# Two loads of an attention decode step, cut differently: W_down's last 96 rows as 93 + 3, the first K as four pieces

## The chip, the cores and the metric

The kernel runs on one core of one Trainium2 chip. The metric is the device time of one execution in microseconds, taken as the median of several executions. The time before is 661.27 us, the median of three runs (660.88 to 662.06).

## The reference

One decode step of a transformer block for two sequences (B = 2, one token each, D = 512): a layer norm, attention with 32 heads of 128 over a cache of 8192 positions, a residual, another layer norm, and a feed-forward part with a ReLU gate. All inputs are bf16.

```python
def _A_ref(x, k_cache, v_cache, wq, wo):              # k_cache, v_cache: (2, 32, 8192, 128)
    q = (x @ wq).reshape(B, Sq, Hq, Dh).transpose(0, 2, 1, 3)
    scores = einsum("bhqd,bhkd->bhqk", q, k) * (Dh ** -0.5)
    p = softmax(scores)
    o = einsum("bhqk,bhkd->bhqd", p, v)
    return o.transpose(0, 2, 1, 3).reshape(B, Sq, Hq * Dh) @ wo

def _B_ref(x, W_gate, W_up, W_down):                  # (512, 1376), (512, 1376), (1376, 512)
    gate = x @ W_gate
    gate = gate * (gate > 0)
    return (gate * (x @ W_up)) @ W_down

h = x + _A_ref(layernorm(x), k_cache, v_cache, wq, wo)
h2 = h + _B_ref(layernorm(h), W_gate, W_up, W_down)
```

(The function bodies are shortened; the output is h2, 2 x 512 in bf16.) The two caches are 256 MB together, and every byte of them is used once.

## The kernel before

**Steps.** The attention runs in N = 32 steps, each with one sequence and two heads. A step loads a K block and a V block of 4 MB each: the 16,384 rows of 128 numbers of two heads, laid on 128 partitions with 128 rows each, so that a partition gets one contiguous stretch of 32 KB. There are two buffers of each kind (`kbuf`, `vbuf`), used in turn. K0 below is the K block of step 0, V31 the V block of step 31.

**A step.** VectorE multiplies the K block with the query, which stands repeated on all partitions (L320), adds up the 128 products by halving (L338, four additions) and a last sum (L342), takes the maximum of each partition (L350) and, after TensorE has spread it (L352), the maximum over the partitions (L276). ScalarE sums 8 of the 128 columns instead of VectorE (L329) and makes the exponentials (L279). TensorE multiplies them with the V block (L378, or L367 in the last two steps). Step 0 multiplies its K block in two halves, so that the first half can start when half of the block is there; for that the load is cut into two pieces (L149, `pieces=2` of `load_kv`, L124 to L131).

**The order of the loads.** All loads but that of x are issued by SyncE (SP), in one queue, in the order of the program. At the front stand W_q (4 MB, into `wbig`), K0 in two pieces, K1 and V0; then in each step i the K block of step i + 2 and the V block of step i + 1 (L396 to L401). Each of these waits for its buffer: a K load for VectorE's last sum of the step that used the buffer, a V load for TensorE. The instructions keep their order, so that a load that waits holds back those behind it. A load also waits for the landing of the eighth load before it, since the loads take turns on eight semaphores.

**The end.** After V31 come W_o in three loads (L412; 2 MB, 1 MB, 1 MB, into `wbig`), W_gate and W_up (L421, 1376 KB each, into the free half of `kbuf`), and W_down. Of W_down's 1376 rows, 1280 lie in `wd_sb`, loaded in three pieces of 768, 256 and 256 KB (L425, with 6, 2 and 2 KB for a partition, in rows of 2 KB), and the last 96 (`LASTW`) in a tile of their own, `wd_r`, one row of 1 KB on a partition (L430). Behind the last step, TensorE multiplies with W_o (L464), W_gate and W_up (L500) and W_down (L533: ten chunks of `wd_sb`, then `wd_r` with four matmuls); VectorE copies the result (L538), TensorE brings it into rows and adds the residual (L539), VectorE rounds it (L541), and SP stores y (L542).

Of the kernel before, what the change touches and what calls it, by code (L numbers as in the profile page):

```python
# [13 lines left out]
def _free(t, offset, dims):  # L14

    return bass.AP(tensor=t.tensor, offset=t.offset + offset, ap=[t.ap[0]] + [list(d) for d in dims])


def _dram(t, offset, dims):
    return bass.AP(tensor=t.tensor, offset=t.offset + offset, ap=[list(d) for d in dims])  # L20
# [3 lines left out]
def kernel(  # L24
# [13 lines left out]
    nc = tc.nc  # L38
    P = nc.NUM_PARTITIONS
    B, Sq, D = A_x.shape  # L40
# [20 lines left out]
    FULL = F // (2 * P) * 2  # L61
    LASTW = F - FULL * P
# [20 lines left out]
    kbuf = big.tile([P, 2, ROW], bf16)  # L83
# [3 lines left out]
    wd_r = big.tile([P, D], bf16)  # L87
# [36 lines left out]
    def load_kv(cache, buf, i, pieces=1):  # L124
        b, g = steps[i]
        w = ROW // pieces
        for k in range(pieces):
            nc.sync.dma_start(  # L128
                out=buf[:, i % 2, k * w:(k + 1) * w],
                in_=_dram(cache, (b * Hkv + 2 * g) * Sk * Dh + k * w, [[ROW, P], [1, w]]),  # L130
            )  # L131
# [13 lines left out]
    with tc.manual_schedule():  # L145

        nc.sync.dma_start(out=wq_all, in_=_dram(A_wq, 0, [[KC * Hq * Dh, P], [1, KC * Hq * Dh]]))  # L147
        nc.scalar.dma_start(out=xrow[0:B, :], in_=_dram(A_x, 0, [[D, B], [1, D]]))
        load_kv(A_k_cache, kbuf, 0, pieces=2)  # L149
        load_kv(A_k_cache, kbuf, 1)  # L150
        load_kv(A_v_cache, vbuf, 0)

# [33 lines left out]
        for c in range(KC):  # L186
            nc.tensor.matmul(
                out=x_ps[:, c, :], lhsT=xrow[0:B, bass.DynSlice(c, P, step=KC)], rhs=ident[0:B, 0:B],
# [13 lines left out]
            out=xn.rearrange("p c b -> p b c"), in0=dev, in1=_free(rstd, 0, [[1, B], [0, KC]]), op=ALU.mult,  # L202
# [204 lines left out]
        for (h0, m, blocks, k, loads), n in zip(SETS, rows):  # L407
            r0 = h0 * Dh
            for p0, w in blocks:
                r = 0  # L410
                for nr in loads:
                    nc.sync.dma_start(  # L412
                        out=wbig[p0:p0 + w, off + r * D:off + (r + nr) * D],
                        in_=_dram(A_wo, (r0 + r) * D, [[n * D, w], [1, nr * D]]),
# [9 lines left out]
        for w in WD:  # L424
            nc.sync.dma_start(  # L425
                out=wd2[:, k0:k0 + w, :],
                in_=_dram(B_W_down, k0 * 2 * P * D, [[2 * D, P], [2 * P * D, w], [1, 2 * D]]),
            )
            k0 += w
        nc.sync.dma_start(out=wd_r[0:LASTW], in_=_dram(B_W_down, FULL * P * D, [[D, LASTW], [1, D]]))  # L430

        scores(N - 1)
        powers(N - 1)
# [6 lines left out]
        for k, (h0, m, blocks, _, _) in enumerate(SETS):  # L440
# [4 lines left out]
            for b in range(B):  # L445
# [4 lines left out]
                for p0, w in blocks:  # L450
                    mb = w // q
                    nc.vector.tensor_tensor(
                        out=_free(sp, p0, [[q, mb], [1, q]]), in0=_free(ocol, h1 * B + b, [[B, mb], [0, q]]),
# [5 lines left out]
        for k, (h0, m, blocks, _, _) in enumerate(SETS):  # L459
            n = rows[k]  # L460
            pn = sum(blocks[-1])
            for r in range(n):
                for c in range(KC):
                    nc.tensor.matmul(  # L464
                        out=att_ps[:, c, :],
# [18 lines left out]
            out=hx, in0=_free(hc, 0, [[1, KC], [KC, B], [0, KC]]), in1=_free(quarter, 0, [[0, KC], [0, B], [1, KC]]),  # L484
# [22 lines left out]
        for c in range(KC):  # L507
            nc.tensor.matmul(
                out=y_ps[0:B * KC, bass.DynSlice(c, P // KC, step=KC)],
# [8 lines left out]
        for r, f in parts:  # L518
            nf = f.stop - f.start
            nc.vector.scalar_tensor_tensor(  # L520
                out=gate[r, f, :], in0=g_ps[r, f, :], scalar=0.0, in1=_free(rvar[r], 0, [[0, nf], [1, B]]),
# [8 lines left out]
        for fc in range(FC):  # L530
            w, src = (P, wd_sb[:, fc, :]) if fc < FULL else (LASTW, wd_r[0:LASTW])
            for c in range(KC):
                nc.tensor.matmul(  # L533
                    out=d_ps[:, :, c], lhsT=src[:, c * P:(c + 1) * P], rhs=hm[0:w, fc, :],
# [38 lines left out]
```

## Time and profile before

| what | value |
|---|---|
| median of three runs | 661.27 us (660.88 to 662.06) |
| the profiled execution | 661.32 us |
| its span, first to last instruction | 659.5 us |
| DVE busy | 591.8 us (90%) |
| PE busy | 334.4 us (51%) |
| ACT busy | 142.2 us (22%) |
| SP's DMA queue q1 | 281.06 MB, 99.0% of 16 engines' span |
| mean rate over the span | 427 GB/s |

The span is what the profile covers; the 1.8 us between it and the execution's own time lie around the first and the last instruction. "Busy" is the time in which an engine executed something. The share of q1 is the time that its packets took, over the span of the 16 DMA engines of the core. A load is cut into packets, one for each contiguous stretch, and the trace has the start, length and bytes of each packet, but not the engine that carried it. On a DMA engine the packets run one after the other.

### The profile page before, as it was taken

To read this page: it belongs to the slowest core of one execution; us is meant where nothing else is said; L and a number is where in the kernel's file an instruction comes from. 1 tells how busy PE (TensorE), PEld (TensorE's weight loads), DVE (VectorE), ACT (ScalarE), POOL (GpSimd) and SP (SyncE) were. 2 spreads that over 40 slices of the span, in tenths; PEclk is the share of its full clock that TensorE was granted. 3 is DMA by queue.
4 is the path that set the end of the run, shared out by engine and by line. 5 is a ranking of instruction groups with operands and counts; after the bars stand their busy time and mean duration, and the time that the engine had idled before them with its cause. 6 is when DMAs were issued, how large, how long until landed. Compare 5 with 4: busy or idle time off the path is not lost.

```text
span 659.5 us, 4819 instructions
## 1 busy us (share of the span) xinstructions
PE 334.4 (51%) x1745; PEld 137.2 (21%) x1745; DVE 591.8 (90%) x302; ACT 142.2 (22%) x695; POOL 6.1 (1%) x35
## 2 busy tenths in 40 slices
PE   2135567653355564435665443665445455553565
PEld 1012222211121221111221111222112122121365
DVE  0899999999999999999999999999999999999941
ACT  2222232222202222211222220122222022222310
POOL 3000000000000000000000000000000000000000
PEclk9998887676778766678776668877677887667855
DMA  8999999999999999999999999999999999999996
GB/s 370 435 435 445 417 441 432 426 441 426 433 438 425 439 433 426 444 423 435 434 427 441 425 434 441 421 439 428 431 443 423 435 441 421 441 424 433 444 409 260
DMA packets 11068, 281.37 MB, mean 427 GB/s; under 512 B 1218, under 2 KB 1316, under 8 KB 1956
## 3 DMA queue, kind: packets, MB, share of 16 engines
q1 hardware_dynamic: 11040, 281.06, 99.0%
q8 instruction: 14, 0.23, 0.1%
q14 instruction: 10, 0.08, 0.0%
q10 hardware_dynamic: 4, 0.00, 0.0%
HBM read 281.05 MB, written 0.00 MB: 426 GB/s over the span
## 4 chain that ended last, share of the span: by engine, by line
DMA 49%; DVE 48%; PE 2%; issue 0%; SPq 0%; ACT 0%; DVEq 0%; ACTq 0%
DMA kbuf<-in_A_k_cache_dram 44%; DVE kbuf L320 23%; DVE kbuf L338 21%; DMA vbuf<-in_A_v_cache_dram 3%; DVE scol L342 3%; DMA kbuf<-in_B_W_down_dram 3%; PE po L378 1%; DVE nm L276 1%; DVE pm L350 0%; ACT pgz L279 0%; SPq L128 0%; PE d_ps L533 0%; SPq L147 0%; PE y_ps L539 0%; DVE y L541 0%
## 5 line engine op out<-in xcount | busy, mean ns | idle before, releaser
L378 PE MATMUL po<-vbuf,pgz 128*8 128x512 bf16 x960 | 273.6, 455 | 264.0 <-ACT pgz L279 264.0
L320 DVE TENSOR_TENSOR kbuf<-kbuf,qrep 128x16384 bf16<-128x16384 bf16 (+2 forms) x33 | 277.2, 8400 | 32.0 <-DMA kbuf<-in_A_k_cache_dram 32.0
L338 DVE TENSOR_TENSOR kbuf<-kbuf 128x7680 bf16<-128x7680 bf16 (+4 forms) x128 | 258.9, 2023 | 3.3
L378 PEld LDWEIGHTS <-pgz 128*8 128x8 bf16 x960 | 92.8, 99 | 435.9 <-ACT pgz L279 263.7
L279 ACT ACTIVATE pgz<-scol,nm 64x128 bf16<-64x128 f32 x64 | 27.9, 436 | 246.6 <-DVE nm L276 246.2
L329 ACT ACTIVATE whole<-kbuf 128x128 f32<-128x128 bf16 x256 | 75.3, 295 | 8.0 <-DVE kbuf L320 7.3
L383 ACT ACTIVATE ob<-po 8x512 f32<-8x512 f32 x30 | 17.6, 587 | 202.3 <-PE po L378 202.3
L329 ACT ACTIVATION_READ_ACCUMULATOR whole<-kbuf 128x1 f32 x256 | 47.8, 187 | 0.0
L342 DVE TENSOR_REDUCE scol<-kbuf 128x120 f32<-128x960 bf16 (+1 forms) x32 | 36.8, 1149 | 1.1
L352 PE MATMUL mx_ps<-nscale,pm 128*128 128x128 f32 x64 | 15.8, 330 | 22.7 <-DVE pm L350 22.6
L352 PEld LDWEIGHTS mx_ps<-nscale,pm 128*128 128x128 f32 x64 | 10.0, 196 | 33.0 <-issue 28.6
L210 PE MATMUL q_ps<-wbig,xn 128*2 128x512 bf16 x32 | 10.7, 469 | 8.3 <-DMA wbig<-in_A_wq_dram 8.3
L279 ACT ACTIVATION_READ_ACCUMULATOR pgz<-scol,nm 64x1 f32 x64 | 11.7, 183 | 0.0
L350 DVE TENSOR_REDUCE pm<-scol 128x1 f32<-128x128 f32 x32 | 9.1, 284 | 2.5
L388 PE MATMUL o_ps<-sel,ob 128*128 128x8 f32 (+1 forms) x64 | 8.4, 258 | 5.5 <-ACT ob L383 5.5
L276 DVE TENSOR_REDUCE nm<-mx_ps 128x2 f32<-128x128 f32 x32 | 9.1, 284 | 0.9 <-PE mx_ps L352 0.9
L214 ACT ACTIVATE qrow<-q_ps 2x512 bf16<-2x512 f32 x8 | 4.7, 586 | 24.2 <-PE q_ps L210 24.2
L388 PEld LDWEIGHTS o_ps<-sel,ob 128*128 128x128 f32 x64 | 7.7, 191 | 9.5 <-ACT ob L383 8.3
L367 PE MATMUL o_ps<-pgz,vbuf 128*128 128x2 bf16 x256 | 7.1, 165 | 5.1 <-ACT whole L329 5.1
L367 PEld LDWEIGHTS <-vbuf 128*128 128x128 bf16 x256 | 7.2, 105 | 5.2 <-DMA vbuf<-in_A_v_cache_dram 5.2
L218 PE MATMUL r_ps<-qrow,pick 2*64 2x256 bf16 x32 | 3.9, 321 | 5.4 <-ACT qrow L214 5.4
L263 DVE RECIPROCAL rz<-o_ps 128x8 f32<-128x8 f32 (+2 forms) x10 | 1.9, 189 | 5.2 <-PE o_ps L367 5.2
(88 smaller groups left out, 64.0 us busy)
## 6 DMA issues: line engine op xcount, KB each, us to landing
vbuf<-in_A_v_cache_dram SPq DMA_DIRECT2D x32, 4096.0 KB, 29.2
kbuf<-in_A_k_cache_dram SPq DMA_DIRECT2D x31, 4096.0 KB, 20.3
wbig<-in_A_wq_dram SPq DMA_DIRECT2D x1, 4096.0 KB, 12.1
kbuf<-in_A_k_cache_dram SPq DMA_DIRECT2D x2, 2048.0 KB, 18.7
wbig<-in_A_wo_dram SPq DMA_DIRECT2D x1, 2048.0 KB, 24.2
wbig<-in_A_wo_dram SPq DMA_DIRECT2D x2, 1024.0 KB, 28.2
kbuf<-in_B_W_gate_dram SPq DMA_DIRECT2D x1, 1376.0 KB, 30.9
kbuf<-in_B_W_up_dram SPq DMA_DIRECT2D x1, 1376.0 KB, 33.9
```

The costliest lines, as they stand in the source:

```text
L210: nc.tensor.matmul(out=q_ps[0:B, :], lhsT=xn[:, c, :], rhs=wq_sb[:, c, n * 512:(n + 1) * 512], start=(c == 0), stop=(c == KC - 1),)
L276: nc.vector.tensor_reduce(out=nm, in_=mx_ps, axis=AXIS.X, op=ALU.min)
L279: nc.scalar.activation(out=pgz[r, s, :, j], in_=scol[r, :], func=ACT.Exp, scale=SCALE, bias=nm[r, j:j + 1], accum_out=zc[r, b, g, j:j + 1],)
L320: nc.vector.tensor_tensor(out=kv, in0=kv, in1=_free(qrep, (b * NG + g) * Dh, [[0, n], [1, Dh]]), op=ALU.mult,)
L329: nc.scalar.activation(out=whole, in_=kt[:, t * Dh:(t + 1) * Dh], func=ACT.Copy, accum_out=scol[:, t:t + 1],)
L338: nc.vector.tensor_tensor(out=lo, in0=lo, in1=_free(kt, half, [[Dh, nv], [1, half]]), op=ALU.add,)
L342: nc.vector.tensor_reduce(out=scol[:, 0:nv], in_=_free(kt, 0, [[Dh, nv], [1, 8]]), axis=AXIS.X, op=ALU.add,)
L352: nc.tensor.matmul(out=mx_ps.rearrange("p a b -> p (a b)"), lhsT=_free(pm, 0, [[0, P]]), rhs=nscale, start=True, stop=True,)
L367: nc.tensor.matmul(out=o_ps[e][:, 2 * k:2 * k + 2], lhsT=vbuf[:, s, t * Dh:(t + 1) * Dh], rhs=pgz[:, s, t, :], start=(t == 0), stop=(t == ...
L378: nc.tensor.matmul(out=po[e][r, :], lhsT=_free(pgz, s * NT * 2 + u * T4 * 2, [[1, 2 * T4]]), rhs=vbuf[:, s, u * T4 * Dh:(u + 1) * T4 * Dh] ...
L383: nc.scalar.activation(out=ob[r, :], in_=po[e][r, :], func=ACT.Copy)
L388: nc.tensor.matmul(out=o_ps[e][:, 0:2 * n], lhsT=ob[:, t * Dh:(t + 1) * Dh], rhs=sel[:, t, 0:n, :], start=(t == 0), stop=(t == T4 - 1),)
```

## The change

The first K block is loaded in four pieces of 1 MB instead of two of 2 MB. The last 96 rows of W_down are loaded in two loads of 93 and 3 rows instead of one of 96. The buffers, the computation and the order of all other loads stay as they are; the first multiplication of step 0 now needs two landings, so does the second, and so do the four matmuls with `wd_r`. The lines behind the second edit move down by four.

```diff
@@ -146,7 +146,7 @@
         nc.sync.dma_start(out=wq_all, in_=_dram(A_wq, 0, [[KC * Hq * Dh, P], [1, KC * Hq * Dh]]))
         nc.scalar.dma_start(out=xrow[0:B, :], in_=_dram(A_x, 0, [[D, B], [1, D]]))
-        load_kv(A_k_cache, kbuf, 0, pieces=2)
+        load_kv(A_k_cache, kbuf, 0, pieces=4)
         load_kv(A_k_cache, kbuf, 1)
         load_kv(A_v_cache, vbuf, 0)
@@ -427,7 +427,11 @@
             k0 += w
-        nc.sync.dma_start(out=wd_r[0:LASTW], in_=_dram(B_W_down, FULL * P * D, [[D, LASTW], [1, D]]))
+
+        for r0, w in ((0, 93), (93, 3)):
+            nc.sync.dma_start(
+                out=wd_r[r0:r0 + w], in_=_dram(B_W_down, (FULL * P + r0) * D, [[D, w], [1, D]]),
+            )
```

## Prediction

> **What bounds the kernel now.** I read the busy times and the slices of the span first, then the chain of waits, then the last stretch by windows of 0.5 us and in order of time. The page says which resource is full:
>
> ```profile
> DMA  8999999999999999999999999999999999999996
> q1 hardware_dynamic: 11040, 281.06, 99.0%
> DMA 49%; DVE 48%; PE 2%; issue 0%; SPq 0%; ACT 0%; DVEq 0%; ACTq 0%
> SPq L128 <- DVE scol L342: 538.8, 30, 19.2
> ```
>
> SP's one queue keeps the 16 DMA engines at 99.0% of the span, so 281 MB of loads set the pace. DVE is 90% busy, but SP waits for DVE (538.8 us in 30 waits) with the next transfer already queued, and in the chain of waits, in order of time, DVE runs without a wait from 22.64 to 110 us and from then on waits for each K load to land:
>
> ```profile
> 1.72 20.90 DMA kbuf<-in_A_k_cache_dram
> 22.64 4.44 DVE kbuf L320
> ...
> 110.65 19.84 DMA kbuf<-in_A_k_cache_dram
> ...
> 635.81 19.41 DMA kbuf<-in_B_W_down_dram
> 655.22 0.04 issue
> 655.26 0.49 PE d_ps L533 x12
> ```
>
> So a nanosecond added to every DMA engine early is a nanosecond at the end, and what lands last before 655.26 sets the end. The last stretch in order of time (start, us, engine, line, tiles):
>
> ```profile
> 654.06 1.01 PE L533 MATMUL d_ps<-hm,kbuf 128*128 128x2 bf16 x32 [0.39 <-DMA kbuf<-in_B_W_down_dram]
> 655.26 0.37 PE L533 MATMUL d_ps<-hm,kbuf 128*128 128x2 bf16 x8 [0.19 <-DMA kbuf<-in_B_W_down_dram]
> 655.50 0.25 PE L533 MATMUL d_ps<-hm,wd_r 96*128 96x2 bf16 x4
> 655.78 0.17 DVE L538 CAST d<-d_ps 128x8 bf16<-128x8 f32 x1 [1.84 <-PE d_ps L533]
> ```
>
> PE waits for the last 256 KB piece of W_down until 655.26 and takes the 96 rows of wd_r at 655.50 without a wait: they were issued at 640.57 and landed 14.8 us later, at 655.4. Their slack is 0.1 us. Only what follows (d, y, the store at 656.62) lies behind.
>
> The windows (busy us of each engine with counts, then PE's clock, the DMA share, GB/s) show that the 16 DMA engines don't finish together:
>
> ```profile
> 650.50:651.00 0.50, 0.50 (x8) 0.40 (x5) 0.00 (x0) 0.00 (x0) 0.00 (x0) 0.50 1.01 402
> 652.50:653.00 0.50, 0.50 (x25) 0.50 (x23) 0.00 (x0) 0.00 (x0) 0.00 (x0) 0.50 0.59 227
> 654.00:654.50 0.50, 0.44 (x16) 0.44 (x17) 0.00 (x0) 0.00 (x0) 0.00 (x0) 0.50 0.43 162
> 654.50:655.00 0.50, 0.50 (x22) 0.49 (x19) 0.00 (x0) 0.00 (x0) 0.00 (x0) 0.50 0.23 80
> ```
>
> 0.59 of 16 is about nine engines still at work, 0.43 is seven. The packet records (start, length and bytes of each packet, without the engine's number) give the same: the 1 KB packets of wd_r come in sixteen runs of six. Six runs start at 651.7 to 652.2 (span time), three at 653.1 to 653.5, and seven late ones at 654.4, five times about 654.8, and 655.15.
>
> **The change, part by part.**
>
> *K0 in four loads.* On one engine, consecutive packets of one load start 607 ns apart for 16 KB, 306 ns for 8 KB and 1209 ns for 32 KB, with 6 ns more between two loads. K0 gives each engine 8 rows of 32 KB: now 2 x (8 x 607 + 6) = 9,724 ns, then 4 x (8 x 306 + 6) = 9,816 ns. That is +0.09 us on every engine, and with the queue full it goes to the end. Bounds: 0, if a pause further on swallows it, to +0.09; I take +0.09. The two added issues on SP cost 1.45 / 3 = 0.48 us each, so K1 and V0 are issued 1.0 us later, at about 3.2 and 3.7 us; W_q's load runs until 12.5 us and K0's until 22.6 ahead of them, which covers it. Without that cover it would be 1.0 us of empty queue. DVE's two first multiplications (L320) wait for two landings each instead of one, the later of which is 0.05 and 0.09 us later than now (17.83 and 22.64); DVE's lead is spent by 110.65, so this costs nothing at the end.
>
> *The waits that shift.* Each load waits for the landing of the eighth load before it. Two more loads at the front move the pairing of the next few loads only: K2 then also waits for W_q and all four pieces of K0, landed by 22.6, and it can't be issued before DVE frees its buffer at 36.59 anyway; V1 waits for x's load, done at 2.1; K3, V2, K4 and V3 wait for a piece of K0 where they waited for W_q, x or K0. From K5 on each load is paired as before. At the end the three W_down pieces wait for K31, V30 and V31, and wd_r's load for the first W_o load, as now. The new 3-row load waits for the second W_o load, and the store of y for the third one instead of the second. SP's wait for the second ended at 643.0, and PE's for the third at 645.45. So the 3-row load is issued at 643.0 to 643.4, over 8 us before any engine comes to it, and only the store (656.62) is queued behind it on SP. Cost 0.
>
> *wd_r in 93 and 3 rows.* Here is the cost. In the records every load gives all its engines the same number of rows: 8 of 128, 6 of 96. Equal shares of 93 whole rows are 31 on three engines or 93 on one. I take three, the nearest to what a load does now, and three for the 3 rows too. Rows of 1 KB start 42 ns apart on an engine. So the three engines get 31 x 42 + 6 + 42 = 1.35 us instead of 6 x 42 = 0.25, and the other thirteen get nothing. For an engine of the early nine this ends by 653.5 + 1.35 = 654.9, before PE comes to these rows at 655.50: cost 0. For the late seven it ends at 655.75, about 656.15, or 656.5; with 0.09 from landing to PE (as the last W_down piece: records 655.17, PE 655.26) PE starts at 655.85, 656.25 or 656.6 instead of 655.50: +0.35, +0.75 or +1.1. The gain on the thirteen relieved engines is bounded by the slack, under 0.1 us, since wd3's landing keeps PE at 655.26. Lower bound of the part 0, upper bound (93 rows on one late engine, 93 x 42 = 3.9 us) +3.4. I take +0.75. PE's four matmuls now wait for two landings; behind them are only d, y and the store.
>
> The Trainium skill, page "DMA: Bandwidth & Descriptors", section "Why a DMA increments its semaphore by 16 and not by 1", states that such a load runs on the largest number of engines up to 16 that divides its slowest dimension, and on the lowest-numbered ones. By that rule 96 rows use 16 engines, as six rows on each here show, and 93 rows and 3 rows both use the same three; it speaks against this change, and by it the sum is the one above, with the uneven and the one-engine outcomes excluded. No run shows it for 93 yet.
>
> Sum: 0.09 + 0.75 = +0.84 us. The profiled execution took 661.32 us (span 659.5 and 1.8 around it), 0.05 above the median 661.27, so it stands for the runs: 661.27 + 0.84 = 662.1.
>
> **The rivals.**
>
> *Hidden.* All engines that get the rows are of the early nine, or the rows are spread unevenly over all. For: nine of sixteen end early, and the three engines whose very first packets start first (2.1 us) end at 651.7, 651.7 and 653.1; if start order is engine order, the rows go there. Against: drawn blindly, three of nine early ones have 9/16 x 8/15 x 7/14 = 15%. Time: 661.27 + 0.09 = 661.4.
>
> *Slower by more.* With three engines instead of 16 the 1 KB rows run at the pitch of a 2 KB row, 80 ns: 31 x 80 = 2.5 us after 654.8 puts PE at 657.4, +1.9 and 0.09: 663.3. With 93 rows on one engine it is +3.4: 664.8. For: every price I have of 1 KB rows is from runs of six. Against: runs of 24 rows of 2 KB hold 80 ns throughout.
>
> *Faster.* The late engines are late because their stream pauses: followed by their spacing, the records show about a dozen pauses of 0.9 us and about as many of 0.3, each followed by a packet that takes 0.25 to 0.55 us longer, so that one of 0.9 costs 1.4 us; engines without one end 3 us early. A changed front could move them. If all seven late engines were spared one pause, the last piece of W_down would land 1.4 us earlier: 659.9. It decides only from the point where not one engine is hit twice; against it, nine of sixteen must stay early and seven change, and 0.09 us more work gives no cause.
>
> *No change in what it does* is excluded: the loads of 8 KB and of 31 rows must show in the packets.
>
> **How the numbers follow.** Chances: forecast 0.52 (its own range 661.5 to 662.8, as the late engines' three prices and the 1.2 us between the runs shown make it), hidden 0.20, slower by more 0.20, faster 0.08. 0.2% is 1.3 us, about what a measurement of this kernel can tell from no change. Faster by over that: the last case, 0.08. Slower by over that: all of the third case and 0.23 of the forecast's 0.52, where a pause or the slowest engine is added to +0.84: 0.43. Within: 0.49. The range leaves out the faster case and the one-engine outcome: 661.0 to 663.4.
>
> **What would show it.** In the packet records, three runs of 31 or 32 packets of 1 KB at 42 ns instead of sixteen of six, and 512 more packets of 8 KB with 256 fewer of 16 KB; K1 landing 0.09 us later; K31's and V31's landings moved by 0.1; PE's wd_r matmuls at L537 now with a wait of 0.4 to 1.1 us for DMA wd_r, and d, y and the store behind it by the same. The prediction is wrong if PE takes wd_r without a wait (hidden), if the 1 KB pitch is not 42 ns, or if W_down's last 256 KB piece lands over 0.5 us earlier or later than before, which nothing here prices.

## The result, and the profile after

The changed kernel takes 662.01 us (median of 22 runs, 661.64 to 662.96), the kernel before 661.18 us (22 runs beside it, 660.65 to 662.06): ratio 1.0014, 95% interval 1.0007 to 1.0020, and the medians differ by +0.83 us. That is a small loss, under 0.2%, and clear of no change. Here and below a ratio leaves out every run that is over 1.5% above the fastest of its kernel (four of the seven of front_93, at 695 to 704 us, and four of the twelve of mid_93, at 675 to 678), while a median is of all runs.

The page of the profiled execution after (busy DMA in 40 slices; DMA queues with packets, MB and share of 16 engines) shows the same full queue, with 278 more packets on it:

```profile
DMA  8999999999999999999999999999999999999996
q1 hardware_dynamic: 11318, 281.06, 99.0%
q8 instruction: 13, 0.21, 0.1%
```

Of the 278, 256 are K0's, in halves. The other 22 are packets of 4 bytes. Their number fits one for each engine that a load uses, in all fourteen profiles of this study: here 32 more for two loads of K0, 16 fewer for the 96 rows, three more for the 93 and three for the 3.

The last stretch in order of time answers to the one shown of before:

```profile
655.45 0.37 PE L537 MATMUL d_ps<-hm,kbuf 128*128 128x2 bf16 x8 [0.24 <-DMA kbuf<-in_B_W_down_dram]
656.78 0.25 PE L537 MATMUL d_ps<-hm,wd_r 96*128 96x2 bf16 x4 [0.95 <-DMA wd_r<-in_B_W_down_dram]
657.06 0.17 DVE L542 CAST d<-d_ps 128x8 bf16<-128x8 f32 x1 [3.24 <-PE d_ps L537]
657.90 0.29 SPq L546 DMA_DIRECT2D out_dram<-y  x1
```

W_down's last 256 KB piece releases PE at 655.45 (655.26 before), but the four matmuls with wd_r, which had no wait, now stand idle for 0.95 us. The store goes out at 657.90 instead of 656.62. The chain of waits (start, us, what) has a new last transfer, counted from the issue of the 3-row load:

```profile
642.98 13.67 DMA wd_r<-in_B_W_down_dram
656.64 0.14 issue
656.78 0.26 PE d_ps L537 x4
```

And the windows show one engine alone at the end (the column before the last is the share of 16 engines; 0.07 is one). The first line is of the kernel before, the others are of the changed one:

```profile
655.50:656.00 0.50, 0.24 (x10) 0.16 (x7) 0.17 (x1) 0.00 (x0) 0.00 (x0) 0.50 0.00 0
654.50:655.00 0.50, 0.45 (x17) 0.36 (x15) 0.00 (x0) 0.00 (x0) 0.00 (x0) 0.50 0.15 57
655.00:655.50 0.50, 0.26 (x9) 0.18 (x7) 0.00 (x0) 0.00 (x0) 0.00 (x0) 0.50 0.07 25
655.50:656.00 0.50, 0.33 (x8) 0.24 (x8) 0.00 (x0) 0.00 (x0) 0.00 (x0) 0.50 0.07 25
656.00:656.50 0.50, 0.00 (x0) 0.00 (x0) 0.00 (x0) 0.00 (x0) 0.00 (x0) 0.50 0.03 8
```

In the packet records the 1 KB packets of wd_r come in three runs of 32, 42.3 ns apart, instead of sixteen of six. They start at 651.59, 651.92 and 654.85. The first two are over at 653.3, long before PE wants the rows; the third ends at 656.22, and PE starts on it 0.56 us later.

The two pages' spans differ by 0.4 us only (659.5 and 659.9), though the stores differ by 1.28. The first profile of before is the odd one: there SP saw the store landed 1.84 us after its issue. In the thirteen other profiles of this study it was 1.19 to 1.22 us.

### The profile page after: what moved, and what is told of

Read it like the earlier page. It is cut to its first block, busy times and chain, and to the rows that moved or that the text cites. A ratio compares the mean times of both kernels' runs of the same rounds, so it can differ in the third digit from the quotient of the medians.

```text
span 659.9 us, 4824 instructions
## 1 busy us (share of the span) xinstructions
PE 336.4 (51%) x1745; PEld 137.9 (21%) x1745; DVE 591.6 (90%) x302; ACT 142.3 (22%) x695; POOL 6.1 (1%) x35
## 4 chain that ended last, share of the span: by engine, by line
DMA 49%; DVE 48%; PE 2%; issue 1%; SPq 0%; ACT 0%; DVEq 0%; ACTq 0%
DMA kbuf<-in_A_k_cache_dram 43%; DVE kbuf L320 23%; DVE kbuf L338 21%; DMA wbig<-in_A_wo_dram 4%; DVE scol L342 3%; DMA wd_r<-in_B_W_down_dram 2%; PE po L378 1%; DVE nm L276 1%; SPq L128 0%; DVE pm L350 0%; ACT pgz L279 0%; SPq L412 0%; SPq L147 0%; PE y_ps L543 0%; DVE y L545 0%
```

## The experiments

The kernel before ran beside each group; its medians were 660.90, 660.93 and 661.09 us. "1 KB runs" are the starts of wd_r's packet runs that have more than six packets, in us of the span.

| kernel | K0 loads | wd_r rows | median us | ratio to before, 95% interval | 1 KB runs |
|---|---|---|---|---|---|
| k0_four_only | 4 | 96 | 660.73 | 0.9996 (0.9987 to 1.0005) | none |
| wdr_93_only | 2 | 93 + 3 | 661.98 | 1.0017 (1.0008 to 1.0026) | 651.5, 651.6, 654.7 |
| wdr_48_48 | 4 | 48 + 48 | 661.05 | 1.0002 (0.9993 to 1.0011) | none |
| wdr_89_7 | 4 | 89 + 7 | 661.17 | 1.0004 (0.9995 to 1.0012) | 651.8 |
| wdr_94_2 | 4 | 94 + 2 | 662.62 | 1.0025 (1.0016 to 1.0034) | 651.7, 654.8 |
| before_again | 2 | 96 | 661.25 | 1.0004 (0.9995 to 1.0013) | none |
| front_96 | 2 | 96, at the front | 661.29 | 1.0025 (1.0002 to 1.0047) | none |
| front_93 | 2 | 93 + 3, at the front | 695.09 | 1.0124 (1.0099 to 1.0149) | 41.4, 41.5, 41.5 |
| mid_96 | 2 | 96, in step 24 | 661.30 | 1.0003 (0.9994 to 1.0011) | none |
| mid_93 | 2 | 93 + 3, in step 24 | 662.84 | 1.0021 (1.0011 to 1.0030) | 525.2, 525.7, 528.7 |
| few_96 | 2 | 96 | 660.72 | 0.9996 (0.9988 to 1.0005) | none |
| few_93 | 2 | 93 + 3 | 661.89 | 1.0014 (1.0006 to 1.0023) | 651.4, 651.7, 654.8 |

**One part alone: k0_four_only and wdr_93_only.** Each is the kernel before with one of the two edits:

```diff
-        load_kv(A_k_cache, kbuf, 0, pieces=2)
+        load_kv(A_k_cache, kbuf, 0, pieces=4)
```

```diff
-        nc.sync.dma_start(out=wd_r[0:LASTW], in_=_dram(B_W_down, FULL * P * D, [[D, LASTW], [1, D]]))
+        for r0, w in ((0, 93), (93, 3)):
+            nc.sync.dma_start(
+                out=wd_r[r0:r0 + w], in_=_dram(B_W_down, (FULL * P + r0) * D, [[D, w], [1, D]]),
+            )
```

> K0 in four loads, wd_r in one load of 96 rows. Theory (the three engines that carry 31 rows each make the loss): +0.1 us against the kernel before (16 x 306 + 2 x 6 more packets' time per engine, 0.09 us), PE takes wd_r at L533 within 0.1 us of the end of the matmuls before it. Rival (the four pieces at the front cost it): about +0.8, as the whole change.

> K0 in two loads, wd_r in 93 + 3 rows. Theory: +0.7 us (the whole change's 0.83 less 0.09), PE waits 0.4 to 1.1 us for wd_r at L533 unless all three engines end early. Rival (K0's pieces): 0.

K0's pieces alone cost nothing that can be told (-0.17 us, interval -0.9 to +0.3); a piece takes 2,453 ns on an engine, four of them 9,812, against 9,725 for two halves, so the 0.09 us are there in the packets. The rows alone make the whole loss, +1.08 us (interval +0.5 to +1.7; +0.7 was expected). Their line in order of time:

```profile
656.61 0.25 PE L536 MATMUL d_ps<-hm,wd_r 96*128 96x2 bf16 x4 [0.84 <-DMA wd_r<-in_B_W_down_dram]
```

**The same count of loads, other rows: wdr_48_48, wdr_89_7 and wdr_94_2.** These keep four loads of K0 and two of wd_r, and change the two numbers of rows only:

```diff
-        for r0, w in ((0, 93), (93, 3)):
+        for r0, w in ((0, 48), (48, 48)):
```

(and (0, 89), (89, 7) and (0, 94), (94, 2) in the other two).

> K0 in four loads, wd_r in two loads of 48 rows: as many loads, waits and semaphores as the changed kernel, but 48 rows can go 3 to each of sixteen engines. Theory: +0.1 us against the kernel before, -0.7 against the changed one; 1 KB packets in runs of three and three on sixteen engines. Rival (one more load with its wait and its issue on SP costs it, or the shifted semaphores): +0.8 as the changed kernel.

> K0 in four loads, wd_r in 89 + 7 rows; 89 is prime, so equal shares of whole rows mean one engine. Theory: one run of 89 packets of 1 KB at 42 ns, 3.8 us on one engine: if that engine is among the late ones PE waits about 3 us for wd_r and the time is +3.2; if it ends 2 to 3 us early, +0.1 to +1. Rival (uneven spread over sixteen, with a dearer landing): +0.8 whatever the rows, and no run longer than six.

> K0 in four loads, wd_r in 94 + 2 rows; equal shares of whole rows are 47 on two engines. In the runs so far two of the three engines of the 93 rows began their wd_r rows at 651.5 to 651.9 us and one at 654.7 to 654.9, and the one engine of the 89 rows at 651.8. Theory (the loss is that one late engine): if it is the third, the two runs of 48 packets start near 651.6, end near 653.7, PE doesn't wait for wd_r, and the time is +0.1 to +0.2 us against the kernel before, though each engine carries half as many rows again as with 93; if it is the second, one run ends near 656.8, and the time is +1.6. Rival (the loss grows with the rows on an engine): above the changed kernel's +0.8 in either case, with a wait for wd_r.

With 48 + 48 no run of 31 appears and the loss is gone (+0.15 us, interval -0.5 to +0.7): neither the further load nor its wait nor the shifted semaphores make it. With 89 rows a single engine takes 90 packets from 651.79 to 655.61, and PE hardly waits; with 94 rows two engines take 48 each, one from 651.73, one from 654.81 to 656.85, and the time is +1.69 us, more than with 93. The two kernels in order of time, 89 + 7 first:

```profile
655.64 0.37 PE L536 MATMUL d_ps<-hm,kbuf 128*128 128x2 bf16 x8 [0.18 <-DMA kbuf<-in_B_W_down_dram]
656.20 0.25 PE L536 MATMUL d_ps<-hm,wd_r 96*128 96x2 bf16 x4 [0.18 <-DMA wd_r<-in_B_W_down_dram]
```

```profile
655.29 0.37 PE L536 MATMUL d_ps<-hm,kbuf 128*128 128x2 bf16 x8 [0.19 <-DMA kbuf<-in_B_W_down_dram]
657.41 0.24 PE L536 MATMUL d_ps<-hm,wd_r 96*128 96x2 bf16 x4 [1.75 <-DMA wd_r<-in_B_W_down_dram]
```

So the wait for wd_r does not grow with the rows on the busiest engine: 89 rows on one cost a wait of 0.18 us, 47 on each of two cost 1.75. It hangs on which engine is among them. A late engine is used by 93 and 94 rows and not by 89. If a smaller set of engines always lies within a larger one, the late engine is the second. The Trainium skill, page "DMA: Bandwidth & Descriptors", section "Why a DMA increments its semaphore by 16 and not by 1", states this choice (the largest number up to 16 that divides the rows, the lowest-numbered engines); the packet runs agree with the numbers, 3 for 93, 1 for 89, 2 for 94, and the late run agrees with sets that lie within each other. Which numbers the engines have no trace shows.

**The same load far from the end: front_96, front_93, mid_96 and mid_93.** wd_r's load is moved behind V0's load at the front, or into the step loop:

```diff
             if i + 1 < N:
                 load_kv(A_v_cache, vbuf, i + 1)
+            if i == 24:
+                for r0, w in ((0, 93), (93, 3)):
+                    nc.sync.dma_start(
+                        out=wd_r[r0:r0 + w], in_=_dram(B_W_down, (FULL * P + r0) * D, [[D, w], [1, D]]),
+                    )
```

> K0 in two loads; wd_r's one load of 96 rows stands at the front, behind V0. Every engine does its six rows (0.25 us) at the front instead of at the end, so W_down's last piece lands 0.25 us later, and PE takes wd_r right behind it: between 0 and +0.25 us against the kernel before, by both theories. It is the base for the next run.

> K0 in two loads; wd_r's loads of 93 and 3 rows stand at the front, behind V0, with 600 us of other loads behind them. Theory (an engine's extra packets stay with it, since its queue never runs empty): the late one of the three engines keeps its 1.1 us (26 more rows x 42 ns) to the end, W_down's last piece lands about 1 us later than with 96 rows at the front, and PE waits for kbuf, not for wd_r: +0.8 to +1.1 against front_96. Rival (a load far from the end is hidden): as front_96.

> wd_r's one load of 96 rows stands in the step loop, behind V25's load, with about 150 us of other loads behind it. Both theories: between 0 and +0.3 us against the kernel before, as with the load at the front, whose profile took wd_r at 655.79. The base for the next run. The long 32 KB packets of the front runs (1359 ns instead of 1213) are not expected; if they appear, they are not bound to the front.

> The same place, with 93 + 3 rows. Theory (extra packets stay with their engine, since its queue never runs empty): the second engine is 26 x 42 ns = 1.1 us later to the end, W_down's last piece lands at about 656.0 in place of 655.2 on the DMA, PE waits for kbuf and not for wd_r, and the time is +0.8 to +1.1 us against mid_96. Rival (far from the end it is hidden): as mid_96.

In step 24, some 130 us before the end, the 93 rows cost as much as at the end: the eight runs of mid_93 that its ratio counts took 662.11 to 663.23 us, and their middle is 1.1 us above mid_96. The last pieces of W_down in the two profiles, mid_96 first:

```profile
656.15 0.37 PE L537 MATMUL d_ps<-hm,kbuf 128*128 128x2 bf16 x8 [0.21 <-DMA kbuf<-in_B_W_down_dram]
656.38 0.25 PE L537 MATMUL d_ps<-hm,wd_r 96*128 96x2 bf16 x4
```

```profile
657.20 0.37 PE L537 MATMUL d_ps<-hm,kbuf 128*128 128x2 bf16 x8 [0.25 <-DMA kbuf<-in_B_W_down_dram]
657.44 0.25 PE L537 MATMUL d_ps<-hm,wd_r 96*128 96x2 bf16 x4
```

PE no longer waits for wd_r, which landed long ago, but for kbuf, 1.05 us later. The windows show that it is one engine again, first two of mid_96, then two of mid_93:

```profile
655.00:655.50 0.50, 0.50 (x21) 0.50 (x22) 0.00 (x0) 0.00 (x0) 0.00 (x0) 0.50 0.15 57
656.00:656.50 0.50, 0.35 (x12) 0.35 (x12) 0.00 (x0) 0.00 (x0) 0.00 (x0) 0.50 0.00 0
```

```profile
655.00:655.50 0.50, 0.50 (x14) 0.49 (x11) 0.00 (x0) 0.00 (x0) 0.00 (x0) 0.50 0.13 49
656.00:656.50 0.50, 0.50 (x21) 0.50 (x22) 0.00 (x0) 0.00 (x0) 0.00 (x0) 0.50 0.06 25
```

The others end no later than in mid_96 (0.13 against 0.15 of 16 still at work), so the 1.05 us are not a slower stream on all engines. The late engine has carried its 26 extra packets through eleven K and V blocks and all the weights behind them. While its queue does not run empty, the late engine makes up nothing of what it is given, 130 us before the end as little as at the end; the two early engines have room for theirs. At the front the base behaved as expected (PE took wd_r at 655.79, right behind the kbuf matmuls of 655.55; its interval is wide since three of twelve runs took 664 to 670 us), but the theory could not be tried there: front_93 took 662.4 to 703.7 us, and in its profile (700.4 us) the packets themselves are longer for most of the time, of which more at the end.

**The program's own packets: few_96 and few_93.** The page lists two queues, q8 and q14, that carry instructions and not data. In the packet records of before, all 19 packets of these two queues between 15 and 632 us stand where one engine's stream of 32 KB packets pauses. It has no other pause of 100 ns or more there, and but for the 19 packets behind the pauses every 32 KB packet in that time took 1,213 to 1,219 ns. So no engine is slow in itself. Six of the 19, with the engine's pause found from the spacing of its packets:

| instruction packet, us | queue, KB | took ns | pause of one engine ns | next packet longer by ns |
|---|---|---|---|---|
| 119.0 | q8, 16 | 967 | 960 | 461 |
| 163.0 | q14, 8 | 309 | 302 | 241 |
| 318.7 | q8, 16 | 879 | 860 | 551 |
| 386.0 | q14, 8 | 309 | 302 | 538 |
| 512.0 | q14, 8 | 309 | 302 | 245 |
| 513.5 | q8, 16 | 936 | 919 | 499 |

So a 16 KB packet holds its engine up by 1.4 us and an 8 KB packet by 0.55 or 0.84. In k0_four_only and wdr_93_only the first eight q8 packets hit eight different engines, and the ninth the first of them again. Of the 13 before the end of the loads, five engines get two and three get one. Six of the ten 8 KB packets hit one engine, three another, and the tenth one that ends early all the same. That makes 6 early engines, 3 with one packet of 16 KB, and 7 late ones, which are the 6, 3 and 7 of the prediction. The Trainium skill, page "Runtime: NRT & Kernel Launch", section "Instruction fetch mechanics", states that an engine's program is refilled in blocks of 16 KiB, 256 instructions, by DMA. By that figure TensorE's 3,490 weight loads and matmuls are an estimated 13.6 blocks; the profiles show 13 or 14 packets on q8. The page calls the cost of a new block mostly hidden. For the DMA engine that carries the block it is not, with the 1.4 us above.

The test makes the program shorter. The two kernels leave out three quarters of the products with V in 30 of the 32 steps:

```diff
-                for u in range(NT // T4):
+                for u in range(NT // T4 // 4):
...
-                        start=(u == 0), stop=(u == NT // T4 - 1),
+                        start=(u == 0), stop=(u == NT // T4 // 4 - 1),
```

> The kernel before, but only the first 8 of the 32 pairs of matmuls of a step (L378) are made; three quarters of the products with V are left out in 30 of the 32 steps, all loads stay. TensorE's program shrinks from 3490 to 2050 loads of weights and matmuls. Theory (the DMA engines end at three different times because packets of 16 KB of program, on queue q8, each hold up one engine by 1.4 us): 13 such packets become about 8, so that none of the eight engines is hit twice; more engines end at 653 to 653.5, and at most the engines hit by the 8 KB packets of q14 remain at 654.5 to 655. Rival (the engines differ in themselves): the ends stay at 6, 3 and 7 engines. The time: -0.3 to 0 us, as one or two late engines are left.

> The same reduced kernel with wd_r in 93 + 3 rows. Theory: if the late second engine is late by two 16 KB program packets, it is now hit once, begins its wd_r rows at about 653.3, ends at 654.7, and PE doesn't wait for wd_r: 0 to +0.2 us against few_96. If it is late by the 8 KB packets of q14, it stays late: +0.8 to +1.1. Rival (that engine is slow in itself): +0.8 to +1.1 as well, and the ends of all engines as before.

The instruction queues in the pages, the first line of the kernel before and the others of few_96, and two windows of few_96:

```profile
q8 instruction: 14, 0.23, 0.1%
q8 instruction: 8, 0.13, 0.1%
q14 instruction: 10, 0.08, 0.0%
```

```profile
652.50:653.00 0.50, 0.50 (x25) 0.50 (x22) 0.00 (x0) 0.00 (x0) 0.00 (x0) 0.50 0.56 213
654.00:654.50 0.50, 0.46 (x17) 0.46 (x18) 0.00 (x0) 0.00 (x0) 0.00 (x0) 0.50 0.14 53
```

Six blocks fewer, and between 654.0 and 654.5 two engines are still at work (0.14 of 16) where before it was seven (0.43). The wd_r runs start at 651.3 to 652.0 for seven, at 652.9 to 653.3 for seven, and at 654.42 and 654.82 for two. So the program's packets make the three groups. The time hardly moves (-0.37 us, interval -0.8 to +0.3), because two late engines are enough to hold the end. In few_93 the late run of 93 rows starts at 654.80 as ever, PE waits, and the time is 1.17 us above that of few_96:

```profile
656.74 0.24 PE L536 MATMUL d_ps<-hm,wd_r 96*128 96x2 bf16 x4 [1.18 <-DMA wd_r<-in_B_W_down_dram]
```

This time alone does not decide, since an engine hit by q14 and an engine slow in itself were both expected at +0.8 to +1.1; what speaks against the second is the even length of the 32 KB packets. With only the q14 engines late, the engine that makes the loss is one of these two; by its start, that of few_96's last, it is the one hit six times. That the rows and the six pauses fall on the same engine is inferred from these starts, since the records don't name engines.

**The kernel before again.**

> The kernel before, once more with a profile. In its first profile the store at 656.62 was seen as landed 1.84 us after its issue, and in the five others so far 1.19 to 1.20 us after. If the long wait belongs to this kernel it is there again, and the end from the store's issue to the last instruction is 2.8 us as before; if it was chance, 2.2 us.

The store was seen as landed after 1.21 us, and from its issue to the last instruction it took 2.17 us, not 2.80: the long wait was chance. Against this profile the change moves the store from 656.69 to 657.90 (+1.21) and the span from 658.9 to 659.9 (+1.0).

No kernel here beats the one before by more than its interval: k0_four_only and few_96 are 0.04% below it, with intervals that reach above it, and few_96 leaves work out.

## Why the prediction was right

It named +0.84 us; +0.83 was measured. The mechanism was the forecast one: three engines get the rows, one of them is late, and PE waits for it. That the two figures agree to 0.01 us is luck. Which engines get the rows was not known, two sizes in the sum were off in opposite directions, and the interval of the runs is +0.5 to +1.3.

- *What bounds the kernel.* Right: the 26 packets added to a late engine came out at the end, both from the end itself and from 130 us before it.
- *K0 in four loads, +0.09.* The packets show it (9,812 against 9,725 ns on an engine). The runs can't resolve it (-0.17 us alone, interval -0.9 to +0.3). DVE's second multiplication started at 23.04 with four pieces alone, but also at 22.99 with the other edit alone, against 22.64, so that shift is mostly between executions.
- *The waits that shift, 0.* Right for the loads: SP began to issue the 3-row load at 642.98, as priced, and no engine came to it before 652.9. The issue itself took 6.5 us instead of 0.35, with nothing behind it but the store, so that it cost nothing. Missed at the end: behind the store SP goes through five semaphores, 62 ns each, and the store's is the second of them in the kernel before and the fifth after. From the store's issue to the last instruction it is 2.16 to 2.18 us with the store second (before_again, front_96, mid_96, few_96), 2.09 to 2.11 with it third (wdr_93_only, front_93, mid_93, few_93), 1.96 with it last (after, wdr_48_48, wdr_89_7, wdr_94_2). In k0_four_only it is the fourth, and the 2.16 there do not fit this row. In the changed kernel it gains 0.2 us, which the sum had at 0.
- *93 and 3 rows, +0.75.* Three engines with 31 rows at 42 ns, a late one among them, early ones hidden: all as written. The size was low. The one late engine is nearly the slowest, not a typical late one, and PE started on wd_r 1.1 us after it could have (656.78 against 655.69, where the matmuls before end their turn), the price that the prediction gave for the slowest engine. The prediction's packet times were 0.3 us too late throughout (654.4, 654.8 and 655.15 should be 654.1, 654.5 and 654.86), and its time from the last packet to PE was too short (0.09 in place of 0.4, and 0.56 for wd_r after the change); in the price the two errors largely cancel.
- *Sum.* 0.09 + 1.1 - 0.2 = +1.0, as the spans against before_again; the medians say +0.83.
- *Hidden.* True for two of the three engines. The guess that engines start in the order of their number did not help: one of the three was late in every profile with 93 rows.
- *Slower by more.* The pitch of 42 ns held in runs of 32, 48 and 90 packets. The price for all rows on one engine (+3.4) took that engine as late; with 89 rows it was an early one, and the cost was +0.27 us (interval -0.3 to +0.8).
- *Faster.* The pauses do not wander. They are the program's own packets, at the same times within some 3 us before and after the change, so that the change spared no late engine one.

## What to carry to other kernels

Give the slowest dimension of a load a count that 16 divides: 93, 94 or 89 rows in place of 96 send the same bytes through 3, 2 or 1 engines at the same 42 ns for each row. In a kernel whose DMA queue never runs empty, such extra work stays with its engine until the end, so look at how far each engine is from the last one, by windows of half a microsecond over the last stretch, before pricing a load that uses few of them. 89 rows on an engine that ended 3 us early were nearly free, and 47 on the late one cost 1.7 us.

## What the runs showed that was not expected

The program itself loads the DMA engines unevenly: 23 or 24 instruction packets, 0.1% of the bytes, make the engines end 3 us apart in the kernels before and after.

An issue on SP is not always 0.3 to 0.4 us. With several loads queued, W_down's second piece took 8.5 us to issue in the changed kernel and 0.34 in the kernel before, its third 2.4 and 3.0, and the 3-row load 6.5. The second piece's issue goes with the number of loads that SP issued before it: 0.33 to 0.34 us with as many as in the kernel before, some 5.4 with one more (front_96, mid_96), 8.5 to 8.6 with two more (after, k0_four_only, mid_93 and the rest). Nothing waited for these; a load behind them that is needed soon would. What holds the issue is not known.

Behind small packets in the middle of the stream the pace can change. In the one profile of front_93 the 32 KB packets, 1,213 ns long in the other kernels but for the few told of here, were some 1,360 ns from 41 us, right behind the 1 KB rows, to about 420 us, and then 1,213 again. The page of that run shows it as a step in the rate:

```profile
GB/s 373 435 406 384 388 382 388 388 387 387 388 388 389 389 389 388 382 388 389 386 388 382 386 387 437 427 436 432 435 432 434 434 429 436 427 441 427 438 415 250
```

16 x 32,768 bytes in 1,360 ns are 386 GB/s. In front_96 no packet behind the 1 KB rows took over 1,236 ns, so that the long packets were seen in one of the two front kernels only. In mid_96 and mid_93 some 19 and 55 packets behind the 1 KB rows took over 1,300 ns, and it passed within 6 us. They were not expected there: it is not bound to the front. That the 1 KB rows are the cause is not shown, and what held it for 380 us in that execution was not settled. In the kernel before and the changed one, where no 1 KB rows stand ahead of 32 KB rows, 19 of the 32 KB packets after the first 15 us took over 1,300 ns, all of them right behind an instruction packet.
